# One of sixteen K loads issued as five DMAs instead of one, with half of its bytes on DMAs of 32 partitions

## The chip, the cores and the metric

The kernel runs on one core of one Trainium2 chip. Its time is the device time of one execution in microseconds (us). Before the change three executions took 200.23, 200.28 and 200.66 us; the median, 200.28 us, is the time that the prediction is about. A further execution was recorded by the hardware profiler and is the source of all durations below.

## The reference

One decode step for eight sequences (one token each): a sliding-window attention over a cache, then a small MLP. Everything is bfloat16.

```python
def _A_ref(x, k_cache, v_cache, wq, wo):          # x: 8 x 1 x 512, caches: 8 x 8 x 8192 x 128
    W = min(4096, max(256, Sk // 4))               # = 2048: only the last 2048 rows are used
    q = (x @ wq).reshape(B, Sq, Hq, Dh).transpose(0, 2, 1, 3)          # 32 heads of 128
    k = jnp.repeat(k_cache[:, :, Sk - W:, :], rep, axis=1)             # 8 K/V groups, 4 heads each
    v = jnp.repeat(v_cache[:, :, Sk - W:, :], rep, axis=1)
    p = softmax(einsum("bhqd,bhkd->bhqk", q, k) * Dh ** -0.5)
    o = einsum("bhqk,bhkd->bhqd", p, v)
    return o.transpose(0, 2, 1, 3).reshape(B, Sq, Hq * Dh) @ wo
def _B_ref(x, w1, w2, w3, w4):
    ...                                            # the w1/w2 branch is identically zero for one token
    x1 = x + hs
    return x1 + gelu(layernorm(x1) @ w3) @ w4

h  = x + _A_ref(layernorm(x), k_cache, v_cache, wq, wo)
h2 = h + _B_ref(layernorm(h), w1, w2, w3, w4)
```

## The kernel before

**Work.** There are 64 items, one for each of 8 sequences and 8 K/V groups. An item has 2048 x 128 of K (512 KB) and as much of V. Together with the weights (wq 4 MB, wo 4 MB, w3 1.8 MB, w4 1.8 MB) the core reads 79.2 MB from HBM once; nothing is read twice.

**Loads.** All loads but the one of x are issued by SyncE (SP), in one program order, on one DMA queue (q1); the helper `dma` at L174 issues them, so they all carry line L176. K comes in sixteen loads of four items each (`load_k`, L337), 2 MB a load, into three buffers of the tile `knat` (`NK = 3`, `KQ = 4`). One load has 128 destination partitions with one run of 16 KB in each: partition 4a+t holds run a of item t, so the source is walked as 32 steps of a, 4 of t, and 16 KB of contiguous bytes. I call the loads K0 to K15; K8 belongs to the items 32 to 35. V comes item by item (`load_v`, L343), 512 KB a load, 128 partitions with a run of 4 KB, into thirteen buffers of `vnat`. Four loads of wo stand between them, and w3 and three pieces of w4 come last.

**What a load waits for.** `load_k` of load j waits on SP until TensorE has transposed the last item of load j-3, which held the same buffer (`e_Thi`, L341). `load_v` waits until the product with V of thirteen items earlier is done (`e_PV`, L346). As SP issues in order, everything behind a waiting load waits too.

**Semaphores.** A load adds 16 to its semaphore. K load j uses `sem_k[j % 3]`, and `K(i)` (L236) gives the value at which the load of item i has landed: 16 for each load on that semaphore so far.

**Compute.** The loop at L392 runs over steps p. In step p TensorE (PE) transposes item p (`pe_T`, L244: 16 transposes, two halves), ScalarE and VectorE evict the two halves (`evict`, L256), PE computes the scores of item p-2 (`pe_QK`, L263), the softmax of a finished sequence is spread over four steps (L277 to L320), and PE multiplies item p-13 by V (`pe_PV`, L322). Only `pe_T` waits for a K load, and only the first of the four items of a load waits long. After the last item the products with wo for the last sequence are mixed with its products with V (`pe_wo_row`, `pe_h0`, `pe_wo`), then come the layer norm, w3 (L475), gelu (`gT`, L500), w4 (L513), a transpose and the store.

The last step before the store therefore needs two things: `gT`, the end of a long chain of computation, and w4, the end of the stream of loads.

Of the kernel before, what the change touches and what calls it, by code (L numbers as in the profile page):

```python
# [14 lines left out]
DH = 128  # L15
G = 8
R = H // G
SK = 8192
W = 2048
W0 = SK - W  # L20
NC = W // 128
# [5 lines left out]
NK = 3  # L27
KQ = 4
# [3 lines left out]
LV = 13  # L32
WO_AT = (15, 23, 31, 39)
NR = 4


class Engine:
# [29 lines left out]
def bass_sequential_preLN__sliding_block_cached__mixer_s_mlp__decode_kernel(  # L67
# [23 lines left out]
    with es:  # L91
# [28 lines left out]
        knat = sb([128, NK, KQ * NC * DH], dt.bfloat16, "knat")  # L120
# [46 lines left out]
        sem_k = [S(f"sem_k{i}") for i in range(NK)]  # L167
# [4 lines left out]
        PE, AC, DV, PO, SP = (Engine(S(n)) for n in ("s_pe", "s_act", "s_dve", "s_pool", "s_sp"))  # L172

        def dma(eng, dst, src, sem, *waits):  # L174
            def f(e):
                e.dma_start(dst, src).then_inc(sem, 16)  # L176
            eng.op(f, *waits, inc=False)
# [55 lines left out]
        e_Tlo, e_Thi, e_lo, e_hi, e_QK, e_PV = {}, {}, {}, {}, {}, {}  # L233
        e_max, e_mT, e_neg, e_negps, e_negc, e_exp, e_PT, e_pT, e_lsel, e_Lb, e_rL, e_scale = ({} for _ in range(12))

        def K(i):  # L236
            return sem_k[i // KQ % NK], 16 * (i // KQ // NK + 1)

        def V(i):
            return sem_v[i % NV], 16 * (i // NV + 1)  # L240
# [3 lines left out]
        def pe_T(i):  # L244
            def half(lo):
                def f(e):
                    for n in range(lo, lo + NC // 2):
                        r = NC * (n % KQ) + NC // KQ * (i % KQ) + n // KQ
                        ins = e.matmul(kT_ps[i % 2][:, n * 128:(n + 1) * 128],  # L249
                                       knat[:, i // KQ % NK, r * DH:(r + 1) * DH], ident_b[:, :], is_transpose=True)  # L250
                    return ins
                return f
            e_Tlo[i] = PE.op(half(0), K(i), e_lo.get(i - 2), e_idb)
            e_Thi[i] = PE.op(half(NC // 2), e_hi.get(i - 2))
# [79 lines left out]
                         e_rL[b], e_oz, *waits)  # L334


        def load_k(i):  # L337
            j = i // KQ
            dma(SP, knat[:, j % NK, :],
                A_k_cache[i // G, i % G:i % G + KQ, W0:SK, :].rearrange("t (a c) d -> a t (c d)", c=KQ * NC),  # L340
                sem_k[j % NK], e_Thi.get(i + KQ - 1 - KQ * NK))  # L341

        def load_v(i):  # L343
            dma(SP, vnat[:, i % NV, :].rearrange("p (c d) -> p c d", c=NC),
# [9 lines left out]
        def pe_wo_row(g):  # L354
            def f(e):
                for r in range(R):
                    h = R * g + r
                    ins = e.matmul(hrow[32 * r:32 * (r + 1), :], oT_all[:, h, :], wo_v[:, h, :],  # L358
                                   start=(g == 0), stop=(g == NR - 1),
                                   tile_position=(0, 32 * r), skip_group_check=True)  # L360
                return ins
            e = PE.op(f, e_sc7[g], e_scale[NB - 2], (sem_wo, 16 * len(WO_AT)))
            if g == NR - 1:

                e = AC.op(lambda e: e.activation(hr[:, 0, :], hrow, ACT.Copy), e)  # L365
                e_wo.append(DV.op(lambda e: e.tensor_tensor(hr[:, 1, :], hrow, hr[:, 0, :], ALU.subtract), e))


        def pe_h0():
            def f(e):  # L370
                for nb in range(KC):
                    e.matmul(hT_ps[:, nb * B:(nb + 1) * B], x_sb[:, nb * 128:(nb + 1) * 128],
                             ident_b[0:B, 0:B], start=(nb == 0), stop=False, skip_group_check=True)
                for part in range(2):
                    for nb in range(KC):
                        ins = e.matmul(hT_ps[:, nb * B:(nb + 1) * B], hr[:, part, nb * 128:(nb + 1) * 128], selb[:, :],
                                       start=False, stop=False, skip_group_check=True)
                return ins
            PE.op(f, e_wo[-1], e_exp[NB - 2], X, e_selb)

        def pe_wo(g):
            def f(e):
                for h in range(R * g, R * (g + 1)):
                    for nb in range(KC):
                        ins = e.matmul(hT_ps[:, nb * B:(nb + 1) * B], wo_v[:, h, nb * 128:(nb + 1) * 128],
                                       oT_all[:, h, 0:B], start=False, stop=(h == H - 1), skip_group_check=True)
                return ins
            e_wo.append(PE.op(f, e_sc7[g]))
# [3 lines left out]
        for p in range(NITEM + LV + 1):  # L392
            if p < NITEM:
                if p % KQ == 0:
                    load_k(p)
                pe_T(p)
                evict(p)
# [20 lines left out]
            i = p - LV  # L418
            if 0 <= i < NITEM:
# [7 lines left out]
                else:  # L427
                    dst = kbank[g % 3][:, 0:R]
# [3 lines left out]
            g = i - 1 - G * LAST  # L432
            if g == NR:
                pe_h0()
            if 0 <= g < NR:
                pe_wo_row(g)
            elif g >= NR:
                pe_wo(g)
# [5 lines left out]
        for n in range(3):  # L444
            lo, hi = W4_AT[n:n + 2]
# [117 lines left out]
```

## Time and profile before

| | |
|---|---|
| Executions | 200.23, 200.28, 200.66 us (median 200.28) |
| Profiled execution | 200.67 us, of which 198.6 us are the span from its first to its last instruction |
| PE busy / weight loads | 158.0 us (80%) / 117.5 us (59%) |
| ScalarE, VectorE, GpSimd busy | 84.7, 70.6, 3.5 us |
| HBM read | 79.18 MB, 399 GB/s over the span |
| Queue of SP's loads (q1) | 97.3% of 16 DMA engines over the span |
| Granted TensorE clock, mean | 0.882 |

The span has a start of its own: the profiled execution is 2.07 us longer than its span, and 0.39 us above the median. DMA engines here are the core's sixteen; the row of q1 adds up the time of all packets and divides by sixteen spans. A packet is one contiguous run of one row, or one completion of 4 bytes.

The trace holds more than the page prints: the start, duration and size of each packet, and the time of each single completion that a load sends to its semaphore. A load with 128 rows sends sixteen of them, one from each engine, when that engine has done its share of eight rows. The prediction uses both kinds of record.

### The profile page before, as it was taken

What the parts mean: (1) busy time and instruction counts of PE and PEld (TensorE: products, weight loads), DVE (VectorE), ACT (ScalarE), POOL (GpSimd) and SP (SyncE); (2) the same over time, 40 slices, a digit from 0 to 9 for tenths busy, and PEclk for the clock granted to TensorE, in tenths of its full rate; (3) what the DMA queues carried; (4) which work ended last, traced back from release to release, by engine and by line L of the source; (5) the groups of instructions that cost most, each with busy time, mean ns of one, the idle gap of its engine ahead of it and who ended that gap; (6) DMA issues with size and microseconds to landing.
All of it is one profiled execution on the core that took longest, in us unless ns stands there. A gap on an engine that the chain in (4) does not pass through costs nothing.

```text
span 198.6 us, 5886 instructions
## 1 busy us (share of the span) xinstructions
PE 158.0 (80%) x2725; PEld 117.5 (59%) x2725; DVE 70.6 (36%) x167; ACT 84.7 (43%) x92; POOL 3.5 (2%) x11
## 2 busy tenths in 40 slices
PE   0037999889999299947999199969997999969853
PEld 0037766567766277635776076747774767556753
DVE  6101545533543033511444024422542344233240
ACT  6001666864574037522465045544554464420330
POOL 7000000000000000000000000000000000000000
PEclk9999999999999669995799969996999699965555
DMA  6999999999999999999999999999999999999970
GB/s 233 449 412 429 426 422 398 422 407 434 412 396 436 406 452 392 414 422 420 429 394 437 406 439 409 449 398 450 395 443 405 443 403 416 419 417 416 404 244 23
DMA packets 18280, 79.56 MB, mean 401 GB/s; under 512 B 1480, under 2 KB 7376, under 8 KB 16080
## 3 DMA queue, kind: packets, MB, share of 16 engines
q1 hardware_dynamic: 18240, 79.18, 97.3%
q8 instruction: 21, 0.34, 0.6%
q14 instruction: 3, 0.02, 0.0%
q10 hardware_dynamic: 16, 0.01, 0.0%
HBM read 79.18 MB, written 0.01 MB: 399 GB/s over the span
## 4 chain that ended last, share of the span: by engine, by line
DMA 66%; PE 28%; SPq 4%; issue 0%; DVE 0%
DMA knat<-in_A_k_cache_dram 56%; PE kT_ps L249 16%; DMA w_sb<-in_B_w_dram 10%; PE S_ps L269 6%; SPq L176 4%; PE oT_ps L327 3%; PE S_ps L513 1%; PE sm L305 0%; PE sm L282 0%; PE sm L317 0%; PE sm L291 0%; PE sm L521 0%; DVE fT L518 0%; DVE out_sb L522 0%
## 5 line engine op out<-in xcount | busy, mean ns | idle before, releaser
L257 ACT ACTIVATE kT_sb<-kT_ps 128x1024 bf16<-128x1024 bf16 x64 | 65.6, 1024 | 89.8 <-PE kT_ps L249 89.8
L249 PE MATMUL kT_ps<-ident_b,knat 128*128 128x128 bf16 x1024 | 76.0, 234 | 18.3 <-DMA knat<-in_A_k_cache_dram 18.3
L249 PEld LDWEIGHTS kT_ps<-ident_b,knat 128*128 128x128 bf16 x1024 | 65.5, 106 | 24.2 <-DMA knat<-in_A_k_cache_dram 19.2
L259 DVE COPY kT_sb<-kT_ps 128x1024 bf16<-128x1024 bf16 x64 | 44.3, 692 | 93.2 <-PE kT_ps L249 93.2
L327 PEld LDWEIGHTS oT_ps<-pT_sb,vnat 128*128 128x128 bf16 x896 | 26.5, 97 | 24.6 <-issue 22.3
L269 PE MATMUL S_ps<-kT_sb,qblk 128*32 128x512 bf16 x256 | 41.1, 611 | 0.0
L327 PE MATMUL oT_ps<-pT_sb,vnat 128*128 128x4 bf16 x896 | 31.3, 165 | 0.0
L295 ACT ACTIVATE P_sb<-S_ps,negcol 128x512 bf16<-128x512 f32 x8 | 11.2, 1401 | 5.9 <-DVE negcol L294 5.9
L269 PEld LDWEIGHTS S_ps<-kT_sb,qblk 128*32 128x32 bf16 x256 | 7.2, 94 | 5.4 <-issue 1.4
L219 PE MATMUL S_ps<-xlnT,wbig 128*128 128x8 bf16 x128 | 3.6, 168 | 7.7 <-DMA wbig<-in_A_wq_dram 7.7
L219 PEld LDWEIGHTS S_ps<-xlnT,wbig 128*128 128x128 bf16 x128 | 3.5, 104 | 7.8 <-issue 7.8
L278 DVE TENSOR_REDUCE mcol<-S_ps 128x1 f32<-128x512 f32 x8 | 5.5, 682 | 1.9 <-PE S_ps L269 1.9
L305 PE MATMUL sm<-ident_b,P_sb 128*128 128x128 bf16 x32 | 3.3, 231 | 2.7 <-ACT P_sb L295 2.7
L327 PEld LDWEIGHTS kT_ps<-pT_sb,vnat 128*128 128x128 bf16 x128 | 4.2, 106 | 1.8 <-issue 1.3
L226 DVE TENSOR_SCALAR qblk<-S_ps 128x32 bf16<-128x32 f32 x8 | 0.9, 182 | 11.1 <-PE S_ps L219 11.1
L309 DVE COPY pT_sb<-sm 128x512 bf16<-128x512 bf16 x8 | 3.3, 417 | 3.4 <-PE sm L305 3.4
L327 PE MATMUL kT_ps<-pT_sb,vnat 128*128 128x4 bf16 x128 | 4.5, 167 | 0.0
L207 PE MATMUL sm<-ident_b,xln_b 8*128 8x8 bf16 x4 | 0.3, 175 | 5.2 <-DVE xln_b L198 5.2
L305 PEld LDWEIGHTS sm<-ident_b,P_sb 128*128 128x128 bf16 x32 | 2.1, 102 | 3.2 <-ACT P_sb L295 3.2
L365 ACT ACTIVATE hr<-kT_ps 128x512 bf16<-128x512 f32 x1 | 0.6, 597 | 6.6 <-PE kT_ps L358 6.6
L317 PE MATMUL sm<-lsel,ones_f 128*128 128x32 f32 x16 | 3.2, 281 | 0.3 <-DVE lsel L313 0.3
L291 PE MATMUL sm<-ones_f,negrow 1*128 1x1 f32 x16 | 3.2, 266 | 0.1
(75 smaller groups left out, 63.2 us busy)
## 6 DMA issues: line engine op xcount, KB each, us to landing
knat<-in_A_k_cache_dram SPq DMA_DIRECT2D x16, 2048.0 KB, 19.1
vnat<-in_A_v_cache_dram SPq DMA_DIRECT2D x64, 512.0 KB, 19.6
wbig<-in_A_wq_dram SPq DMA_DIRECT2D x1, 4096.0 KB, 12.3
wbig<-in_A_wo_dram SPq DMA_DIRECT2D x4, 1024.0 KB, 21.6
w_sb<-in_B_w_dram SPq DMA_DIRECT2D x1, 1792.0 KB, 17.9
w_sb<-in_B_w_dram SPq DMA_DIRECT2D x1, 1280.0 KB, 20.1
w_sb<-in_B_w_dram SPq DMA_DIRECT2D x1, 384.0 KB, 17.5
w_sb<-in_B_w_dram SPq DMA_DIRECT2D x1, 128.0 KB, 7.6
```

Source lines behind the costliest of these rows:

```text
L176: e.dma_start(dst, src).then_inc(sem, 16)
L219: ins = e.matmul(S_ps[0][:, h * B:(h + 1) * B], wq_v[:, kc, h * DH:(h + 1) * DH], xlnT[:, kc * B:(kc + 1) * B], start=(kc == 0), stop=(kc ...
L249: ins = e.matmul(kT_ps[i % 2][:, n * 128:(n + 1) * 128], knat[:, i // KQ % NK, r * DH:(r + 1) * DH], ident_b[:, :], is_transpose=True)
L257: e_lo[i] = AC.op(lambda e: e.activation(kT_sb[:, i % NKT, 0:W // 2], kT_ps[i % 2][:, 0:W // 2], ACT.Copy), e_Tlo[i], e_QK.get(i - NKT))
L259: e_hi[i] = DV.op(lambda e: e.tensor_copy(kT_sb[:, i % NKT, W // 2:W], kT_ps[i % 2][:, W // 2:W]), e_Thi[i], e_QK.get(i - NKT))
L269: ins = e.matmul(S_ps[b % 2][32 * u:32 * (u + 1), :], qblk[:, b, g - g % KQ + t, :], kT_sb[:, i % NKT, :].rearrange("p (n t) -> p t n", t= ...
L278: e_max[b] = DV.op(lambda e: e.tensor_reduce(mcol[:, :], S_ps[b % 2][:, :], AX.X, ALU.max), e_QK[G * b + G - 1], e_mT.get(b - 1))
L291: e_negps[b] = PE.op(lambda e: e.matmul(sm[:, NEG], negrow[0:1, :], ones_f[0:1, 0:1], start=True, stop=True), e_neg[b], e_ones)
L295: e_exp[b] = AC.op(lambda e: e.activation(P_sb[:, j, :].rearrange("p (c a w) -> p c w a", c=4, w=KQ), S_ps[j][:, :].rearrange("p (c w a) - ...
L305: ins = e.matmul(pT_ps[:, jt * 128:(jt + 1) * 128], P_sb[:, j, 128 * jt:128 * (jt + 1)], ident_b[:, :], is_transpose=True)
L309: e_pT[b] = DV.op(lambda e: e.tensor_copy(pT_sb[:, j, :, :].rearrange("p (q jt) h -> p q jt h", jt=4), pT_ps[:, 0:NC * H].rearrange("p (jt ...
L327: ins = e.matmul(dst, vnat[:, i % NV, c * DH:(c + 1) * DH], pT_sb[:, b % 2, (c + NC // KQ * (i % KQ)) % NC, R * g:R * (g + 1)], start=(c = ...
```

## The change

K8 is issued as five DMAs, the fifteen other K loads as before. The first DMA brings the first 8 KB of each of the 128 runs of 16 KB. The other four bring the second 8 KB, each for 32 destination partitions: their source is walked as 8 steps of a, 4 of t, and 8 KB. Only the first of the five waits for the buffer; the others follow it on SP. All five count on the semaphore of K8 (`sem_k[2]`), so `K(i)` adds 64 for K8 and for the later loads on that semaphore (K11 and K14). Bytes, buffers and the order of everything else stay.

```diff
+K8 = 8
 ...
         def K(i):
-            return sem_k[i // KQ % NK], 16 * (i // KQ // NK + 1)
+            j = i // KQ
+            return sem_k[j % NK], 16 * (j // NK + 1 + (4 if j >= K8 and j % NK == K8 % NK else 0))
 ...
         def load_k(i):
             j = i // KQ
-            dma(SP, knat[:, j % NK, :],
-                A_k_cache[i // G, i % G:i % G + KQ, W0:SK, :].rearrange("t (a c) d -> a t (c d)", c=KQ * NC),
-                sem_k[j % NK], e_Thi.get(i + KQ - 1 - KQ * NK))
+            src = A_k_cache[i // G, i % G:i % G + KQ, W0:SK, :].rearrange("t (a c) d -> a t (c d)", c=KQ * NC)
+            dst = knat[:, j % NK, :]
+            if j == K8:
+                m = KQ * NC * DH // 2
+                dma(SP, dst[:, 0:m], src[:, :, 0:m], sem_k[j % NK], e_Thi.get(i + KQ - 1 - KQ * NK))
+                for lo in range(0, 32, 8):
+                    dma(SP, dst[KQ * lo:KQ * (lo + 8), m:], src[lo:lo + 8, :, m:], sem_k[j % NK])
+            else:
+                dma(SP, dst, src, sem_k[j % NK], e_Thi.get(i + KQ - 1 - KQ * NK))
```

## The prediction

> **What bounds the kernel now.** I read the page first: how busy the DMA engines are, the queues, the chain that ended last.
>
> ```profile
> DMA  6999999999999999999999999999999999999970
> q1 hardware_dynamic: 18240, 79.18, 97.3%
> q8 instruction: 21, 0.34, 0.6%
> q10 hardware_dynamic: 16, 0.01, 0.0%
> DMA 66%; PE 28%; SPq 4%; issue 0%; DVE 0%
> ```
>
> The loads fill all sixteen engines to the end (digits of 9), and two thirds of the chain is DMA. So what counts is which engine finishes last. Two small rows matter. q8 fetches instructions: 21 packets, 16 KB each. q10 is the load of x: 8 rows of 1 KB. It has 16 packets, 8 rows and 8 completions, so a load walked in 8 steps runs on 8 engines, not 16. The count of q1 fits 16 for all the rest: 16,800 data packets and 90 loads x 16 completions are 18,240.
>
> Next the chain in order of time and the timeline of its end.
>
> ```profile
> 142.68 21.14 DMA knat<-in_A_k_cache_dram
> 163.82 0.05 issue
> 163.87 1.07 PE kT_ps L249 x16
> ...
> 174.12 20.07 DMA w_sb<-in_B_w_dram
> 194.19 0.14 issue
> 194.33 1.65 PE S_ps L513 x56
> ```
>
> ```profile
> 163.87 1.07 PE L249 MATMUL kT_ps<-ident_b,knat 128*128 128x128 bf16 x16 [0.47 <-DMA knat<-in_A_k_cache_dram]
> ...
> 193.75 0.39 ACT L500 ACTIVATE gT<-g_x 128x56 bf16<-128x56 f32 x2
> 194.33 1.64 PE L513 MATMUL S_ps<-gT,w_sb 128*128 128x8 bf16 x56 [1.60 <-DMA w_sb<-in_B_w_dram]
> ```
>
> The end has two parents, nearly level. The first piece of w4 lands at 194.19 and releases L513. But the first half of gT is ready about 193.95 (half of 0.39 us after 193.75), and gT is the end of a chain in which PE last waited for a DMA at 163.87, for K15. Earlier w4 alone can win 0.25 us; K15's landing moves everything.
>
> Last, the records of single completions (us after the load's first), the eight quickest engines and the eight slowest:
>
> ```
> K8  first  88.20: 0 .03 .21 .29 .30 .34 .55 .94 | 1.57 1.62 1.68 1.79 1.85 1.89 2.16 2.54
> K15 first 159.90: 0 .22 .30 .32 .35 .56 .58 .95 | 2.98 3.03 3.07 3.23 3.25 3.29 3.56 3.93
> w4  first 188.89: 0 .15 .31 .36 .51 .58 .86 .94 | 2.88 2.96 3.21 3.28 4.46 4.67 4.96 5.31
> ```
>
> Eight engines stay together, eight fall behind in jumps. Each jump begins in a q8 fetch: at 18.51 us a fetch of 0.94 us starts, one engine starts its next K packet 0.92 us late, and that packet takes 1.107 instead of 0.611 us, 1.42 us lost in all. Only eight engines ever lose this way. Following packets from the start, the first three to lose are all among those whose first packet of wq began at 1.93 to 2.08 us. The load of x ran at 1.71 to 2.34 us, and the eight other first packets of wq fit right behind its eight. So I take it that the engines of x are the quick ones.
>
> **The change part by part.**
>
> *Bytes per engine.* K8 now gives each engine 8 rows x 16 KB = 128 KB. The first of the five DMAs gives each of 16 engines 8 rows x 8 KB. Each of the other four is walked in 8 steps, like the load of x; if they run on its 8 engines, each of these takes another 4 x 4 x 8 KB = 128 KB. So eight engines move 192 KB, eight 64 KB. Packets follow one another every 155.5 ns (4 KB) and 607.5 ns (16 KB), so I estimate 306 ns for 8 KB by a straight line. The eight with more: 24 x 0.306 + 5 completions x 0.009 = 7.39 us instead of 4.87, +2.52. The others: 2.46 us, -2.41. [...]
>
> *If that is all.* K15 lands at the later of 159.90 + 0.945 + 2.52 = 163.36 and 163.82 - 2.41 = 161.41: 0.46 us earlier. gT is at 193.49; w4 at 188.89 + 0.944 + 2.52 = 192.35. L513 starts 0.14 us after gT, at 193.63 instead of 194.33: -0.70 us.
>
> *Where the bytes land.* Two of the four DMAs write partitions 64 to 127. In every other load sixteen engines take eight rows each, and a 16 KB packet has 611 ns as its minimum and its median however far the engines have drifted: each writes partitions of its own, and none hinders another. Now eight engines bring 2 x 4 x 8 KB = 64 KB each into partitions that the other eight are filling with V at that moment. No row shows two engines at the same partitions. Bounds: nothing lost, or the two share one path. The nearest row for two streams on one path is the packet behind a fetch, 1.107 against 0.611 us, a rate of about half. At half, 64 KB take 4.90 instead of 2.45 us: the eight with more lose 2.45 us again (+4.97 in all), and the others give back what they won (-2.41 + 2.45 = +0.04). Unequal sharing changes only the first number: if the newcomers always go first it is +2.52, if they get a third 64 KB take 7.35 us and it is +7.42.
>
> [...]
>
> I take half: streams that meet on one path are what the trace prices, and these must meet, since neither side ever pauses. K15 then lands at 159.90 + 0.945 + 4.97 = 165.81, +1.99 us. w4 lands at 194.80, gT at 193.95 + 1.99 = 195.94, L513 starts at 196.08: +1.75 us. On the span 198.6 becomes 200.35; on the median, 200.28 becomes 202.03.
>
> *Four more issues on SP.* They go out at the place of K8:
>
> ```profile
> 78.19 0.82 SPq L176 DMA_DIRECT2D knat<-in_A_k_cache_dram  x1
> 79.06 2.02 SPq L176 DMA_DIRECT2D vnat<-in_A_v_cache_dram  x4
> 81.12 0.55 SPq L176 DMA_DIRECT2D knat<-in_A_k_cache_dram  x1
> 81.71 1.54 SPq L176 DMA_DIRECT2D vnat<-in_A_v_cache_dram  x3
> ```
>
> An issue takes 0.4 to 0.6 us (four V in 2.02), so four V loads, K9 and all behind it go out some 2 us later. The quickest engine still had work until 83.34 (the V load before K8), 5.15 us after 78.19, and K8 itself adds over 2.4 us to each, so no engine runs dry: nothing. Were that cover gone, it would be up to 2 us.
>
> *PE in the middle.* PE waited 3.88 us for K8 and 4.45 us for K10, so K8 landing 3.4 us later (88.20 + 0.935 + 4.97 = 94.11 against 90.74) is absorbed before K11. K9 to K14 each land with the same eight engines, +1.9 to +2.5 us, and all reach the end through K15.
>
> *The clock.* The granted clock is 1.0 from 158.6 to 175.7 us and 0.5 after; the final chain starts in one and ends in the other. If its start moves 2 us and the drop does not, up to 1 us of full-clock work becomes 2 us; if the drop moves too, nothing. I take nothing and widen the range.
>
> **The rivals.** *Balance* (other side): the eight with more do not meet the others' writes. Price -0.70 us, 199.58. It decides if 64 KB into the far half cost less than 2.45 + 0.46 = 2.91 us, as then K15 is not later. For it: eight quick engines and 5.31 us of lag at w4, of which 2.52 against 2.41 is nearly the right cure; against: the partitions.
>
> *The eight with more are the laggards*, my matching of x and wq being wrong: K15 at 3.93 + 2.52 behind, +2.52 us; L513 at 196.61, +2.28 us, 202.56; with the meeting +4.97 at K15, 205.0. Against: three of three laggards on the other side, one chance in ten at random (56 of 560 triples).
>
> *Not what it says*: each of the four spreads over 16 engines, or by partition. Bytes stay even: 200.28. Against: q10 shows eight.
>
> **How the numbers follow.** Meeting 0.60, balance 0.20, laggards 0.10, not what it says 0.10. The likeliest gives 202.03. Its own range is 200.3 (newcomers first) to about 203.4 (share between a half and a third, or the clock). With balance, 199.58 with 0.2 for its sum, the range goes from 199.4 to 203.4; left out are 205.0 and a third's share or less, about 0.15. The measurement can tell 0.2%, 0.40 us, from no change. Faster: most of balance, with some unevenness, 0.20. Same: not what it says and newcomers first, 0.13. Slower: the rest, 0.67.
>
> **What would show it.** q1 should count 18,240 + 128 + 4 x 8 = 18,400 packets; 18,432 would be sixteen engines. 8 KB packets of K8 into partitions 64 to 127, and V packets beside them, should take about twice their time; all at 0.31 and 0.159 us would be balance. K8's last completion should come near 94.1, K15's near 165.8 and gT two microseconds later; balance has K15 at 163.4. If K15 moves and the end does not, my last chain is wrong. Engines that pause after 85 us would make the issues the cause.

## The result and the profile after

The changed kernel takes 206.50 us (median of four executions, 206.29 to 206.54) against 200.27 us; the ratio is 1.0305, interval 1.0287 to 1.0323. The direction was forecast, the size was not: 202.0 was predicted, 203.4 was the top of the range. The profiled execution took 206.52 us with a span of 204.5 us, 5.8 us more than before.

The page after, the same rows as before, with the rate in 40 slices of 5.1 us:

```profile
GB/s 245 462 385 439 420 423 388 443 397 436 409 412 418 425 421 398 423 284 289 418 377 384 412 435 412 434 407 441 407 445 400 448 401 413 422 416 417 385 170 4
q1 hardware_dynamic: 18400, 79.18, 96.4%
DMA 56%; PE 35%; SPq 3%; DVE 2%; ACT 2%; issue 1%; ACTq 0%
```

q1 counts 18,400 packets, as forecast for loads on eight engines. The rate falls to 284 and 289 GB/s in the two slices from 87 to 97 us, where K8 is. The share of DMA in the chain is smaller and that of PE larger, because w4 no longer stands at the end.

The chain in order of time and the end of the timeline:

```profile
146.22 23.05 DMA knat<-in_A_k_cache_dram
169.27 0.05 issue
169.31 1.89 PE kT_ps L251 x16
```

```profile
169.31 1.89 PE L251 MATMUL kT_ps<-ident_b,knat 128*128 128x128 bf16 x16 [2.07 <-DMA knat<-in_A_k_cache_dram]
...
199.83 0.39 ACT L509 ACTIVATE gT<-g_x 128x56 bf16<-128x56 f32 x2
200.13 1.65 PE L522 MATMUL S_ps<-gT,w_sb 128*128 128x8 bf16 x56 [1.33 <-ACT gT L509]
```

K15 lands at 169.27 instead of 163.82 us (+5.45), and L522 (L513 before) starts at 200.13 instead of 194.33 (+5.80). It now waits for gT, no longer for w4: the end hangs on K15 alone, as the prediction had it. K8's own last completion came at 96.43 us, where the prediction had 94.1, and PE waited 9.67 us for it (3.88 before):

```profile
96.47 1.89 PE L251 MATMUL kT_ps<-ident_b,knat 128*128 128x128 bf16 x16 [9.67 <-DMA knat<-in_A_k_cache_dram]
```

Busy time by stretch. The columns are the stretch, its length, busy time of the five engines, the granted clock, the DMA share and GB/s; a number behind an x counts instructions. A packet counts in the stretch in which it begins, with all its time and bytes, so the share can pass 1. Of 88 to 95.5 us, first before, then after:

```profile
88.00:95.50 7.50, 4.71 (x56) 3.88 (x56) 0.69 (x1) 1.86 (x2) 0.00 (x0) 0.66 1.02 421
```

```profile
88.00:95.50 7.50, 0.00 (x0) 0.00 (x0) 0.00 (x0) 0.00 (x0) 0.00 (x0) 0.64 1.04 244
```

The DMA engines are as busy as before (1.04 against 1.02) and move little more than half as much. They do not pause, their packets take longer. From 89 to 95 us the packet records give medians of 575 to 644 ns for 8 KB (309 before 88 us) and 284 to 331 ns for the 4 KB of V (159). None of the 4 KB packets takes less than 249 ns there. With each packet's bytes spread over its time, the total stays between 207 and 237 GB/s in each microsecond. The "rate" below is meant so, unless a row of the profile is shown.

Two details stand in the same records. The sixteen engines begin K8 in two groups, at 83.07 to 84.15 us and at 84.34 to 85.43 us. The eight engines of the 32-partition DMAs are six of the first group and the two that begin the second, both at 84.34 us: two of the eight are laggards, engines that are behind. And these two are still on the second DMA, into partitions 32 to 63, where such DMAs alone slow nothing (e1, 309 ns a packet), when the rate falls; their 8 KB packets that begin after 88.6 us take 573 to 622 ns all the same.

### The profile page after: what moved, and what is told of

Same layout as the page of the kernel before. It is cut to its first block, busy times and chain, and to the rows that moved or that the text cites. A ratio compares the mean times of both kernels' runs of the same rounds, so it can differ in the third digit from the quotient of the medians.

```text
span 204.5 us, 5890 instructions
## 1 busy us (share of the span) xinstructions
PE 156.8 (77%) x2725; PEld 116.2 (57%) x2725; DVE 70.6 (35%) x167; ACT 84.7 (41%) x92; POOL 3.5 (2%) x11
## 3 DMA queue, kind: packets, MB, share of 16 engines
q1 hardware_dynamic: 18400, 79.18, 96.4%
## 4 chain that ended last, share of the span: by engine, by line
DMA 56%; PE 35%; SPq 3%; DVE 2%; ACT 2%; issue 1%; ACTq 0%
DMA knat<-in_A_k_cache_dram 56%; PE kT_ps L251 16%; PE S_ps L271 7%; PE oT_ps L329 4%; SPq L177 3%; PE kT_ps L329 2%; PE kT_ps L367 1%; PE S_ps L394 1%; PE sm L307 1%; PE S_ps L522 1%; ACT P_sb L297 1%; ACT L509 1%; PE sm L319 1%; PE sm L284 0%; PE sm L293 0%
## 5 line engine op out<-in xcount | busy, mean ns | idle before, releaser
L251 PE MATMUL kT_ps<-ident_b,knat 128*128 128x128 bf16 x1024 | 74.7, 232 | 25.9 <-DMA knat<-in_A_k_cache_dram 25.9
L251 PEld LDWEIGHTS kT_ps<-ident_b,knat 128*128 128x128 bf16 x1024 | 64.3, 104 | 31.8 <-DMA knat<-in_A_k_cache_dram 26.8
L284 PE MATMUL sm<-ident_f,mcol 128*1 128x128 f32 x16 | 3.0, 270 | 0.3 <-DVE mcol L280 0.3
```

Source lines behind the costliest of these rows:

```text
L251: ins = e.matmul(kT_ps[i % 2][:, n * 128:(n + 1) * 128], knat[:, i // KQ % NK, r * DH:(r + 1) * DH], ident_b[:, :], is_transpose=True)
```

## The experiments

Two questions were open: what makes the packets slow, and why K15 is so much later than by that alone. The runs take the kernel before and add or split one thing at K8. "Spare" is a tile of 8 KB a partition that nobody reads. The ratios compare with runs of the kernel before on the same chip; "K15" is its last completion in the profiled run (163.82 us before).

**e1, two more DMAs into partitions 0 to 63.**

```diff
+            if j == 8:                      # behind the whole K8; m = half a run
+                for lo in (0, 8):
+                    dma(SP, spare[KQ * lo:KQ * (lo + 8), :], src[lo:lo + 8, :, m:], sem_ex)
```

> K8 is loaded whole, as before; behind it two more DMAs of 32 partitions and 8 steps bring its second 8 KB again, for partitions 0 to 63, into a tile that nobody reads. 64 KB more on each of eight engines, 0.5 MB more in all. Theory 'far': only rows in partitions 64 to 127 slow the stream. Then the 8 KB packets take 309 ns, the rate stays above 415 GB/s, and the eight engines are 2.45 us later; two of them are laggards, so K15 and the end come about 2.4 us later: 202.7 (202.2 to 203.0). Theory 'eight': any load on eight engines slows all sixteen. Then 8 KB packets take about 610 ns, the rate is about 210 GB/s for 5 us, 205 to 206.

Ratio 1.0096 (1.0069 to 1.0123), about +1.9 us; K15 at 165.67. Every 8 KB packet but one takes 309 ns, and the rate stays at 416 GB/s or more in each microsecond from 88 to 93. So here eight engines with more bytes slowed nobody. The 2 us are the bytes themselves: at the end of K8 the records show sixteen engines in two groups, 88.07 to 88.81 and 89.44 to 89.83 us, and the eight with more bytes are six of the first group and two of the second.

**e2, the same into partitions 64 to 127** (`for lo in (16, 24)`).

> The same two DMAs for partitions 64 to 127. Theory 'far': 8 KB packets of about 610 ns, all sixteen engines at about 210 GB/s for 5 to 7 us, so 2.45 us for the bytes and 2.5 to 3.5 us for the half rate: 205.2 to 206.3. Theory 'eight': the same time as with partitions 0 to 63, within 0.3 us.

Ratio 1.0257 (1.0197 to 1.0317), K15 at 169.50: as late as with the change itself (169.27). The stretch from 91 to 93 us, for e1 and then for e2:

```profile
91.00:93.00 2.00, 0.83 (x9) 0.21 (x6) 0.69 (x1) 0.89 (x1) 0.00 (x0) 0.55 1.02 418
```

```profile
91.00:93.00 2.00, 0.00 (x0) 0.00 (x0) 0.00 (x0) 0.00 (x0) 0.00 (x0) 0.50 0.97 201
```

418 against 201 GB/s, counted by the packets that begin there, with the DMA share nearly the same. Same bytes, same number of engines: the half of the partitions decides.

**e7, rows of the far half into the near one** (`spare[... lo ...]` from `src[lo + 16:lo + 24]`). As e2 also read other rows of K, this tells source from destination.

> As the run with two more DMAs of 32 partitions into partitions 0 to 63, but they read the rows that belong to partitions 64 to 127. Theory 'place' (where the rows land decides): 8 KB packets of 309 ns, full rate, about 202. Theory 'source' (which rows of K are read decides): 8 KB packets of about 610 ns, half rate, 205 to 206.

Ratio 1.0085 (1.0048 to 1.0123), K15 at 165.95, nearly all packets of 309 ns, and full rate from 91 to 93 us:

```profile
91.00:93.00 2.00, 2.00 (x20) 1.58 (x18) 0.23 (x1) 1.02 (x1) 0.00 (x0) 0.50 1.02 420
```

The destination decides.

**e9, the far half alone.** The two DMAs of e2 go first of all, and wq waits for them.

```diff
+        for lo in (16, 24):
+            dma(SP, spare[KQ * lo:KQ * (lo + 8), :], src[lo:lo + 8, :, m:], sem_ex)
-        dma(SP, wq_v, A_wq..., sem_wq)
+        dma(SP, wq_v, A_wq..., sem_wq, (sem_ex, 32))
```

> The two DMAs of 32 partitions into partitions 64 to 127, moved to the very start; the load of wq waits until they have landed, so eight engines write the others' partitions while nothing else is loaded (but x). Theory 'meeting' (two loads at the same partitions): 8 KB packets of 309 ns, apart from the first ones of the kernel. Theory 'path' (an engine is slow on partitions that are not its own, alone or not): about 610 ns. The time is that of the kernel before plus the wait, 206 to 210, and says little.

205.51 us in its one execution, a little under what was expected of the wait. After the first two packets of each engine all take 309 ns; from 4 to 5 us the eight engines move 213 GB/s. So partitions 64 to 127 are no slow place for these engines. It takes a second load there at the same time.

**e4, even bytes, uneven places.** K8's second half in two DMAs of 64 partitions and 16 steps.

```diff
-                for lo in range(0, 32, 8):
-                    dma(SP, dst[KQ * lo:KQ * (lo + 8), m:], src[lo:lo + 8, :, m:], sem_k[j % NK])
+                for lo in range(0, 32, 16):
+                    dma(SP, dst[KQ * lo:KQ * (lo + 16), m:], src[lo:lo + 16, :, m:], sem_k[j % NK])
```

> K8's first 8 KB as one DMA of 128 partitions, the second 8 KB as two DMAs of 64 partitions and 16 steps: all sixteen engines get the same bytes, but while the first of the two runs all write partitions 0 to 63, and while the second runs 64 to 127. Theory 'far' (rows that meet other engines' rows in one half of the partitions): about half rate for 0.5 MB twice, 4.9 us instead of 2.45, all engines 2.45 us later: 202.6 (202.0 to 203.2). Theory 'eight': sixteen engines, even bytes, so 200.3.

Ratio 1.0124 (1.0082 to 1.0166), K15 at 165.97. The rate is 216 to 281 GB/s from 87 to 92 us. By the 16 steps I take it that no engine has more bytes than another here; no count of packets shows it. The +2.15 us at K15 are less than the 2.53 that the low rate alone comes to (table below), which leaves nothing over for bytes: the price is that of the meeting.

**e3, split but on sixteen engines** (two DMAs of 128 partitions).

> K8 as two DMAs of all 128 partitions, 8 KB a row each: split, but on sixteen engines. Both theories: 8 KB packets of 309 ns, no drop of the rate, 200.3 (200.0 to 200.6). If the issues on SP or the shorter rows were the cause: 201 or more.

Ratio 0.9982 (0.9954 to 1.0009), packets of 309 ns. Rows of 8 KB instead of 16, and one more issue, cost nothing that can be measured.

**e5, four engines into the far half** (one DMA, 16 partitions, `for lo in (16,)`, 4 steps).

> K8 whole, and behind it one more DMA of 16 partitions (64 to 79) and 4 steps, 8 KB a row, into the unread tile: four engines bring 32 KB each into partitions that four others fill. Theory 'pairs' (two engines share what each pair writes): eight engines at half rate, eight at full, so about 320 GB/s, and packets of 4 KB in two groups, 159 and about 310 ns. Theory 'all' (any meeting slows every engine): about 210 GB/s, hardly a packet at 159 ns while it lasts. It takes some 2.5 us in both; time 200.5 to 202.5.

Ratio 1.0085 (1.0046 to 1.0124), K15 at 165.36. Of 62 packets of 4 KB that began between 88.5 and 91 us, four took 159 ns; the median is 276. Four engines with 32 KB each slow nearly everything:

```profile
89.00:91.00 2.00, 0.00 (x0) 0.00 (x0) 0.00 (x0) 0.00 (x0) 0.00 (x0) 0.61 0.88 205
```

205 GB/s by the packets that begin there, 236 with their bytes spread over their time, and not 320: "pairs" falls, and "all" is near. That agrees with the two laggards of the change that were slow in partitions 32 to 63.

**e10 and e8, half the meeting.** e10 is e2 with one DMA of two. e8 is the change with its last two DMAs in one of 64 partitions.

> K8 whole, and one DMA of 32 partitions (64 to 95) and 8 steps into the unread tile, half of what the run with partitions 64 to 127 brought. Theory 'all', cost by bytes: half rate for about 3.5 us instead of 7, so 1.2 us for the bytes and 1.75 us for the rate: 203.3 (202.7 to 203.9). If any meeting cost the same: 205.5 or more.

> The change with its last two DMAs in one of 64 partitions and 16 steps: partitions 64 to 127 get their second 8 KB from all sixteen engines, so eight engines bring 32 KB each into the others' half, instead of 64. Theory 'place' (cost in proportion to the bytes that land in the others' half): half rate for some 3.5 us instead of 7, 32 KB less on the eight engines: 200.3 + 1.2 + 1.8 = 203.3 (202.6 to 204.0). If any meeting costs the same whatever its size: 206.

e10: ratio 1.0164 (1.0064 to 1.0264), K15 at 166.62. e8: 1.0146 (1.0081 to 1.0210), K15 at 166.74. The rate is low for 4.75 and 4.5 us, against 7.5 in e2 and 6.75 in the change: less than all, more than half. It ends only when the last of the engines is through: 8 KB packets were under way from 87.98 to 92.80 us in e10, and from 87.99 to 95.50 us in e2.

**e6 and e11, fewer engines, near half.** e1 with 6 steps (24 partitions a DMA), and with 2 steps (8 partitions).

> K8 whole, and two more DMAs of 24 partitions (0 to 23 and 32 to 55) and 6 steps, so six engines bring 64 KB more each and none meets another. Theory 'six of eight': the two laggards among the eight engines of a 32-partition DMA are not among the first six, so the six have 3 us to spare at K15: 200.3 (200.0 to 200.8), K15's last completion as before. Theory 'any': a laggard is among the six, and the time is that of the run with 32 partitions (0 to 63), about 2 us above the kernel before.

> K8 whole, and two more DMAs of 8 partitions (0 to 7 and 32 to 39) and 2 steps into the unread tile: two engines bring 64 KB more each, into partitions of their own. Theory 'laggard' (bytes cost only on an engine that is already behind): the records show whether one of the two is a laggard when K8 ends. If neither is, K15's last completion stays within 0.3 us and the time is 200.3 (200.0 to 200.7); if one is, K15 and the time come 1.8 to 2.5 us later. Theory 'any' (0.1 MB more anywhere costs its share of the whole stream): 0.3 us in both cases.

e6: ratio 1.0102 (1.0076 to 1.0128). My "six of eight" was wrong, there is a laggard among the first six. At K15 it shows as one completion at 165.73 us, 2.18 us after the fifteenth. e11: ratio 0.9999 (0.9981 to 1.0018), K15 at 164.21. The two engines ended K8 at about 88.08 and 88.28 us, in the quick group, and 64 KB more on each cost nothing that the executions can tell (the interval reaches +0.36 us). K15's 0.39 us lies a little over what "laggard" allowed and near the 0.3 us of "any", and e3's -0.51 shows that single profiles differ by as much, so e11 alone does not tell the two apart. e6 does: its 0.39 MB, spread over the whole stream, would be 0.93 us at 422 GB/s, and K15 came 1.90 us later.

The sixteen completions of K15 show it engine by engine (us after the first, as in the prediction's records):

```
K15 e1  first 160.37: 0 .06 | 2.17 2.25 2.29 2.48 2.75 2.76 2.77 2.80 2.88 2.89 2.95 2.96 | 5.17 5.30
K15 e6  first 160.80: 0 .01 .11 | 1.87 2.03 2.06 2.43 2.49 2.50 2.54 2.56 2.60 2.63 2.68 2.75 | 4.93
K15 e11 first 160.22: 0 .08 .13 .40 .57 .78 | 2.35 2.72 2.78 2.82 2.90 2.91 2.92 3.08 3.11 3.99
```

Before, eight were quick and eight some 3 us behind. A quick engine with 64 KB more drops back by some 2.45 us into the middle group, and a laggard with 64 KB more comes last, beyond 4.9 us. So the engines with more bytes were six quick ones and two laggards in e1, five and one in e6, two and none in e11. In these runs 64 KB more were free, within the 0.4 us that can be told, on two engines with time to spare (e11, +0.39 us at K15), and with a laggard among the engines they cost 1.85 to 2.13 of their 2.45 us (e1, e6, e7).

## Why the prediction was wrong

The terms can be read on K15. "Lost" adds up, over quarters of a microsecond with under 330 GB/s, the share missing to 422 GB/s. "Bytes" is 2.45 us (2.52 with the change) for 64 KB more on a laggard, half for 32 KB.

| run | bytes | lost | sum | K15 measured |
|---|---|---|---|---|
| change | 2.52 | 3.20 | 5.72 | +5.45 |
| e2, far | 2.45 | 3.45 | 5.90 | +5.68 |
| e1, near | 2.45 | 0 | 2.45 | +1.85 |
| e7, near from far rows | 2.45 | 0 | 2.45 | +2.13 |
| e6, six engines near | 2.45 | 0 | 2.45 | +1.90 |
| e4, cross | 0 | 2.53 | 2.53 | +2.15 |
| e10, one far | 1.23 | 2.07 | 3.30 | +2.80 |
| e8, mix | 1.23 | 2.01 | 3.24 | +2.91 |
| e5, four far | 1.23 | 1.04 | 2.27 | +1.54 |
| e3, two | 0 | 0 | 0 | -0.51 |
| e11, pair | 0 | 0 | 0 | +0.39 |

Two terms give every row within 0.8 us, and mostly 0.2 to 0.6 too much, which I leave open; single profiles differ by about half a microsecond (e3).

Against that, step by step:

- *The eight engines are the quick ones: wrong, and the largest error.* I inferred it from three laggards and the start times of wq's packets. The starts fit only loosely: of the eight that I gave to x's engines, three (1.780, 2.230 and 2.344 us) begin 3 or 4 ns before a completion packet of x ends, as packets that follow one another on one engine do (16 KB: 611 ns each, one every 607.5); the other five do not. The runs show six quick ones and two laggards among the eight. With that, the meeting moves K15 by the laggards' full +4.97 us and not by the +1.99 of the engine that was last among the quick: 2.98 us missed. The price was on record, as the rival *the eight with more are the laggards* "with the meeting", 205.0, but I took the eight as all or none, and gave it a tenth.
- *The meeting: right in kind, too small.* Half rate was the likeliest case, and the packets have it: 575 to 644 ns for 8 KB. But I let each engine lose 2.45 us while its own rows met others. In fact all sixteen lose until the last one is through: 6.75 us of low rate, 3.20 us lost, 0.75 us more.
- *Bytes per engine: right.* 18,400 packets and eight engines a DMA. That all four DMAs use the same eight was my assumption. Chains of packets that follow one another show it in part: those from 83.07 and 83.64 us have eight packets of 8 KB and then three groups of four, each with its completion, before they are lost in the meeting. That these are the engines of x no run shows. The 306 ns that I estimated for an 8 KB packet shows as the usual spacing at full rate; each takes 309 ns.
- *The end hangs on K15: right.* But the 0.25 us that I took off for w4's slack did not come back. From K15's landing to the start of the last w4 products it took 30.86 us against 30.51. K15's first sixteen transposes ran at a granted clock of 0.50 (169 to 171 us; 1.00 before, 163.87 to 164.93) and took 1.89 instead of 1.07 us; the rest of the chain was a little quicker. I had taken nothing for the clock and only widened the range. 0.35 us more in place of 0.25 less makes the term 0.60 us.
- *The issues on SP: no cost, but not for my reason alone.* The five issues took 3.88 us. But one V load later held SP until 106.82 us (102.11 before), and K10 behind it went out at 106.87 instead of 102.15:

```profile
78.08 3.88 SPq L177 DMA_DIRECT2D knat<-in_A_k_cache_dram  x5
91.04 15.78 SPq L177 DMA_DIRECT2D vnat<-in_A_v_cache_dram  x1
106.87 0.94 SPq L177 DMA_DIRECT2D knat<-in_A_k_cache_dram  x1
```

  From 105 to 108.5 us the DMA share is 0.90 against 1.11, first before, then after:

```profile
105.00:108.50 3.50, 3.50 (x69) 2.50 (x68) 1.46 (x3) 1.45 (x3) 0.00 (x0) 1.00 1.11 452
105.00:108.50 3.50, 2.91 (x46) 1.98 (x46) 1.25 (x3) 2.93 (x4) 0.00 (x0) 1.00 0.90 313
```

  Some engines did run dry. They were the ones ahead: sixteen completions lay 7.55 us apart at K9 and 4.83 us at the V load behind the next wo. The last engine needed 7.57 us between those two, for loads that cost 7.72 us by the packets of before, so it did not pause. This loss fell on engines with time to spare.

The sum at L522: 1.74 forecast (1.99 less 0.25), 2.98 for the laggards, 0.75 for the meeting, 0.60 for the tail, less 0.27 that the table does not explain, are 5.80 us, as measured. The medians are 6.23 us apart; the profiled execution of before was itself 0.39 us above its median.

**Open.** Why a meeting also slows engines that take no part in it was not shown, only that it does (e5: 58 of 62 packets of 4 KB took more than 159 ns). Nor do the runs tell which numbers the laggards have, or whether the set is the same in each execution: two were found among the eight in the change and in e1, one among six in e6, one among four in e5. The packet records name neither the engine nor the partitions. I read the slow loads as those that bring new engines to a half of the partitions (e2, e4, e5, e8, e10 and the change); none was made to let engines swap rows within one half, so whether the half or the exact rows decide is not shown. No version faster than the kernel before came out of this: an engine with time to spare can only take over rows that others write, and the loads that brought such rows to partitions 64 to 127 made K15 1.54 to 5.68 us later (e5, e10, e2).

## What to carry to other kernels

When a stream of loads binds, ask of each load not only how many engines it uses, but also into which partitions its rows go. Two DMAs of 32 partitions left the stream at 418 GB/s here when they wrote partitions 0 to 63 (e1), and brought it to 201 when they wrote 64 to 127 beside the other loads (e2), until the last row was through. Moving bytes between engines can pay only if the receivers are known to be ahead, which single completions show, and not an argument about their numbers: 64 KB more cost nothing that the executions could tell on two quick engines (e11, ratio 0.9999), and with one laggard among six K15 came 1.90 us later (e6). And when two cases can hold for part of the engines each, the slowest engine decides: price the mixture, not only the pure cases.

## What the runs showed of the hardware that was not expected

Four engines with 32 KB each for partitions 64 to 79, beside the loads of K and V, brought the whole stream from 410 GB/s (87 to 88 us) to 205 (89 to 91 us), or 236 with the bytes of each packet spread over its time (e5), while eight engines alone in the far half moved 213 GB/s at full packet speed (e9). And an instruction fetch of 16 KB cost the engine that it fell on 1.42 us of loading in the profile of before, read at the one of 18.51 us. Eight such fetches began before K8 landed and sixteen before K15, and eight engines of sixteen were then some 1.6 to 2.5 and 3.0 to 3.9 us behind the quickest: the counts fit one and two fetches for each of these eight. They are the laggards that set the end.
